# Two engines with priority for the first down projection's evictions, a three-operand token norm and urgent splits of v

## The chip, the cores and the metric

The kernel runs on one core of a Trainium2 chip. The core has a matrix engine (TensorE, "PE" in the profile, its weight loads "PEld"), a vector engine (VectorE, "DVE"), an activation engine (ScalarE, "ACT"), a general engine (GpSimd, "POOL") and a queue engine that only starts DMAs here (SyncE, "SP"). They share an on-chip memory with 128 partitions, and a smaller accumulation memory (PSUM) into which TensorE writes, in eight banks of 128 x 512 float32. The metric is the device time of one execution in microseconds. Before the change it is 1038.46 us, the median of three runs from 1038.11 to 1038.9.

## The reference

Eight batches of eight heads, 576 tokens, head width 64, go through causal attention with a window of 128 tokens and a bias that falls linearly with distance. The heads side by side make 4608 rows of 512 numbers, and these go through a bilinear feed-forward layer:

```python
scores = np.matmul(q, k.transpose(0, 1, 3, 2)) / np.sqrt(D)
rel = pos[:, None] - pos[None, :]
scores = np.where((rel >= 0) & (rel < 128), scores - slopes * np.abs(rel), -1e9)
attn = np.exp(scores - scores.max(-1)); attn = attn / (attn.sum(-1) + 1e-9)
x = (attn @ v).transpose(0, 2, 1, 3).reshape(4608, 512)
out = ((x @ w_a) * (x @ w_b)) @ w_out        # w_a, w_b: 512 x 1536, w_out: 1536 x 512
```

All inputs and the output are float32. The kernel keeps float32 accuracy by writing an operand as the sum of two float16 numbers, a high and a low half, and by adding three products of halves.

## The kernel before, in words

Work goes batch by batch. Tokens lie along the free axis as two halves of 288 (HT), and the 512 model columns as four blocks of 128 partitions (NPAIR and NE are both 4: four pairs of heads, four blocks of output rows). The 1536 hidden columns are twelve blocks (NF). While TensorE does the feed-forward layer of batch b, the attention of batch b+1 is woven into it.

**The first batch** has a path of its own. `first_attention` computes batch 0's attention while the weights arrive, and the generators `up_weights` and `down_weights` put the weights into form in between: operations on int32 and float32 columns (L100 to L161) that end with the halves in `wup` and `wdn`. At the end of `first_attention`, a pair's part of x is multiplied by its normalisation (L600), squared (`square_x`, L404 to L411), and the four pairs' squares go to `hidden_scale` (L488 to L505): two matmuls with ones per operand (L496, one for 512 tokens and one for 64) sum the squares over partitions into the PSUM tiles `n_ps`; maxima of these give `st.g`, the power of two that scales the hidden values. In `square_x` POOL adds the squares of pairs 1 and 2 onto those of pair 0 (L409), and those of pair 3 stay a second operand.

Then `first_batch` weaves `first_up` (twelve blocks, four groups of twelve matmuls each, L805, evicted by ACT at L758 and by DVE at L760, where DVE needs `st.g`) and `first_down` with the attention of batch 1 and with the rest of the weights. `first_down` goes over the two halves of tokens (t = 0, 1): four PSUM banks `dn_ps` collect 36 matmuls each (L787), in turns, so that all four are finished at almost the same time. Then each is scaled by `oi` and written to a `row` tile by ACT (L791) and sent to memory by a DMA that ACT issues (L792). `row` has two buffers. The five banks that `bank()` hands out in turns hold the next `dn_ps` tiles, and after t = 1 the `up_ps` tiles of batch 1.

**Order of work.** Until the end of `first_batch` only SP's order is written out by hand; the other engines' is set by a scheduler, which takes what is ready by a modelled time and by priority (`tc.high_priority(offset=PRIO)` moves work ahead, PRIO is 2000). From batch 1 on TensorE's order is the program's too. An engine executes its queue strictly in order: an instruction that waits holds up everything behind it, DMA issues included.

**Other names.** `split_v` (L279) makes `vhl`, the two halves of v for a pair of heads: ACT the high half (L282) and DVE the low one (L283); the matmuls L482 multiply it with the transposed probabilities `pT` into `x_ps`. `sc_ps` are scores (L361), `t` and `mn` their reduction by DVE (L369) and exponential by ACT (L370), `phl` the normalised halves (L382, L383), `qkh`, `qkl` the halves of q and k (L308, L325), `vsq` the squares of the next batch's v (L265). PSUM pools: `ps_at`, three banks, holds `sc_ps`, `n_ps`, the weight norms `wn_ps` and small sums; `ps_ef` (three) and `ps_ch` (two) the rest. `rc` tiles (three buffers) hold hidden values.

Of the kernel before, what the change touches and what calls it, by code (L numbers as in the profile page):

```python
# [13 lines left out]
BF16 = mybir.dt.bfloat16  # L14
# [3 lines left out]
AF = mybir.ActivationFunctionType  # L18
ALU = mybir.AluOpType
# [27 lines left out]
def attention_then_bilinear_ffn(ctx: ExitStack, tc: tile.TileContext, qT, kT, vP, w_a, w_b, w_out, rel, slopes2, outT):  # L47
# [231 lines left out]
    def split_v(st, p):  # L279

        vhl = work.tile([P, 2, VCOLS], F16, tag="vhl", name="vhl", bufs=2)
        act.activation(vhl[:, 0, :], st.v[:, p, :], AF.Copy, scale=st.sv)  # L282
        vec.scalar_tensor_tensor(out=vhl[:, 1, :], in0=st.v[:, p, :], scalar=st.sv, in1=vhl[:, 0, :], op0=ALU.mult, op1=ALU.subtract)  # L283
        return vhl

    def load_plain_qk(b, p):
# [110 lines left out]
            act.activation(x[:, c:c + w], ps[:, 0:w], AF.Copy, scale=scale)  # L397
        square_x(p, st, x)

    def square_x(p, st, x, add=True):  # L400

        if p == 0:
            act.activation(st.xq, x, AF.Square, scale=1.02)
            st.squares = [st.xq]  # L404
        else:
            sq = work.tile([P, S], BF16, tag="sq", name="sq")
            act.activation(sq, x, AF.Square, scale=1.02)  # L407
            if add:
                pool.tensor_tensor(out=st.xq, in0=st.xq, in1=sq, op=ALU.add)  # L409
            else:  # L410
                st.squares.append(sq)  # L411

    B12 = 7

# [90 lines left out]
    def first_attention(weights, rate):  # L505
# [74 lines left out]
        def pv(p, pt):  # L580
# [18 lines left out]
            for n, (c, w) in enumerate(halves_of_x):  # L599
                vec.scalar_tensor_tensor(out=x[:, c:c + w], in0=xp[n][:, 0:w], scalar=st.sv, in1=r[:, c:c + w], op0=ALU.mult, op1=ALU.mult)  # L600
            yield
            square_x(p, st, x, p < NPAIR - 1)
            yield

        bias(0)
# [142 lines left out]
    def new_hidden():  # L748
        return work.tile([P, 2, HT], F32, tag="rc", name="rc", bufs=3)
# [29 lines left out]
    def first_down(b, oi, h):  # L779

        started["down"] = b
        for t in range(2):
            pss = [bank("dn_ps") for _ in range(NE)]
            for f in range(NF):
                for e in range(NE):
                    for n, (wi, hi) in enumerate(((0, 0), (0, 1), (1, 0))):
                        pe.matmul(pss[e][:, 0:HT], wdn[:, f, wi, e * P:(e + 1) * P], h[:, f, t, hi, :], start=(f == 0 and n == 0), stop=(f == NF - 1 and n == 2))  # L787
                yield
            for e in range(NE):
                o = row()  # L790
                act.activation(o, pss[e][:, 0:HT], AF.Copy, scale=oi)  # L791
                act.dma_start(outT[e * P:(e + 1) * P, b * S + t * HT:b * S + (t + 1) * HT], o)  # L792

    def row():
        return work.tile([P, HT], F32, tag="row", name="row", bufs=2)
# [234 lines left out]
```

## Time and profile before

| what | value |
| --- | --- |
| three runs | 1038.11, 1038.46, 1038.9 us |
| the profiled execution | 1035.06 us, of which its span is 1033.3 us |
| mean granted TensorE clock | 0.98 |
| PE busy | 980.7 us, 95% of the span |
| DVE busy | 677.4 us, 66% |
| ACT busy | 647.5 us, 63% |
| POOL busy | 315.6 us, 31% |

Times inside the program are microseconds from the span's start. A row of the timeline gives the start, the busy time, the engine, the line and operation, what is written from what, and how many instructions the row holds; square brackets at its end give the idle time of that engine before the row and what ended it. A row of a table by stretches gives the start and end of the stretch, its length, each engine's busy time (with its count of instructions), the granted TensorE clock as a share of full speed, and the DMA engines' share and rate. By stage, `first_attention` ends at about 66 us, `first_up` runs to about 172 us (the last eviction of `up_ps` at L758 begins at 171.6 us), the evictions of `first_down` begin at 193.1 and at 221.4 us, and from 235 us on batches 1 to 7 run.

### The profile page before, as it was taken

The page shows a single profiled execution, that of the slowest core. Times are in us where ns is not written, and L with a number is a line of the kernel's source. Part 1 is how long each engine was busy: PE and PEld are TensorE (multiplying, and loading weights), DVE is VectorE, ACT ScalarE, POOL GpSimd, SP SyncE. Part 2 cuts the span into 40 slices and gives each one's busy share as a digit, 9 for nine tenths or more (in the row PEclk, how much of TensorE's full clock was granted, in tenths as well). Part 3 has the DMA queues.
Part 4 walks back from the last instruction along what each step waited for, and adds up shares of the span by engine and source line. Part 5 has one row for each costly group of instructions (what it writes and reads, how often), then busy time and mean ns, then how long its engine had stood idle before and what let it go on. Part 6 is the DMA issues. An engine that isn't in the chain of part 4 may idle for free.

```text
span 1033.3 us, 23882 instructions
## 1 busy us (share of the span) xinstructions
PE 980.7 (95%) x9325; PEld 754.8 (73%) x9325; DVE 677.4 (66%) x1880; ACT 647.5 (63%) x1672; POOL 315.6 (31%) x348
## 2 busy tenths in 40 slices
PE   8789979889999899889999999999999999999998
PEld 6556657667777677667777777777777778787776
DVE  5889988355778656985767667765776576534430
ACT  7977778556667756667666676667666765423321
POOL 3544562000368205880222212321223012221100
PEclk8899989999999999999999999999999999999999
DMA  8335733462543532435434743453624732200001
GB/s 344 125 111 195 251 86 73 100 155 58 123 88 86 145 74 56 87 80 153 88 65 86 184 90 65 88 116 115 124 52 99 173 65 42 48 31 11 1 13 35
DMA packets 148433, 102.83 MB, mean 100 GB/s; under 512 B 120032, under 2 KB 128352, under 8 KB 147296
## 3 DMA queue, kind: packets, MB, share of 16 engines
q1 hardware_dynamic: 138816, 91.77, 35.8%
q10 hardware_dynamic: 9504, 9.54, 2.9%
q8 instruction: 73, 1.20, 0.5%
q14 instruction: 40, 0.33, 0.1%
HBM read 48.33 MB, written 9.44 MB: 56 GB/s over the span
## 4 chain that ended last, share of the span: by engine, by line
PE 58%; DVE 15%; DMA 12%; ACT 7%; issue 3%; POOL 3%; SPq 2%; ACTq 0%; DVEq 0%; POOLq 0%
PE ch L805 16%; PE p L805 13%; PE dn_ps L901 11%; PE up_ps L805 10%; PE x_ps L482 4%; DMA pT<-phl 3%; DVE phl L383 3%; PE sc_ps L365 2%; DVE t L369 2%; ACT phl L382 1%; DMA v<-in_vP 1%; DMA qk<-in_kT 1%; DMA qst<-qkl 1%; DMA qst<-qkh 1%; DMA qkl<-qkl 1%
## 5 line engine op out<-in xcount | busy, mean ns | idle before, releaser
L805 PEld LDWEIGHTS <-wup 128*128 128x128 f16 x4212 | 407.7, 98 | 126.9 <-issue 18.6
L901 PE MATMUL dn_ps<-h,wdn 128*128 128x288 f16 x2016 | 256.8, 287 | 2.5 <-DVE h L799 2.5
L805 PE MATMUL ch<-xs,wup 128*128 128x288 f16 x1584 | 230.0, 287 | 6.7 <-DVE rc L865 4.3
L901 PEld LDWEIGHTS <-wdn 128*128 128x128 f16 x2016 | 193.9, 98 | 56.6 <-issue 3.7
L805 PE MATMUL up_ps<-xs,wup 128*128 128x288 f16 x1440 | 188.1, 289 | 6.0 <-ACT row L791 3.7
L805 PE MATMUL p<-xs,wup 128*128 128x288 f16 x1188 | 178.7, 287 | 0.0
L860 POOL TENSOR_TENSOR rc<-rc,row 128x288 f32<-128x288 f32 x66 | 64.5, 978 | 254.0 <-DVE row L858 235.6
L370 ACT ACTIVATE t<-t,mn 128x192 f32<-128x192 f32 (+2 forms) x252 | 107.4, 428 | 38.6 <-DVE mn L369 36.9
L383 DVE SCALAR_TENSOR_TENSOR phl<-t,rin,phl 128x192 f16<-128x192 f32 (+2 forms) x252 | 103.9, 447 | 34.5 <-ACT phl L382 34.5
L798 ACT CAST h<-rc 128x576 f16<-128x576 f32 x96 | 64.3, 669 | 64.0 <-DVE rc L865 33.1
L382 ACT ACTIVATE phl<-t,rin 128x192 f16<-128x192 f32 (+2 forms) x252 | 88.6, 426 | 19.4 <-DMA pT<-phl 11.4
L799 DVE TENSOR_TENSOR h<-rc,h 128x576 f16<-128x576 f32 x90 | 72.2, 802 | 26.4 <-ACT h L798 25.9
L369 DVE CUSTOM_DVE_ANT_0 t<-sc_ps,bias,neg 128x192 f32<-128x192 f32 (+2 forms) x216 | 74.3, 389 | 13.4 <-PE sc_ps L365 9.6
L842 ACT ACTIVATE row<-ch,g 128x288 f32<-128x288 f32 x66 | 32.9, 498 | 66.0 <-PE ch L805 66.0
L417 DVE TENSOR_TENSOR xs<-v,xs 128x576 f16<-128x576 f32 x51 | 52.5, 1044 | 28.4 <-ACT xs L416 27.9
L135 POOL TENSOR_TENSOR wup<-wup,wdn 128x512 int32<-128x512 int32 x36 | 56.9, 1602 | 33.7 <-issue 5.6
L906 ACT ACTIVATE row<-dn_ps,oi 128x288 f32<-128x288 f32 x56 | 27.7, 495 | 60.4 <-PE dn_ps L901 60.4
L837 DVE TENSOR_TENSOR rc<-p,rc 128x288 f32<-128x288 f32 x66 | 30.0, 454 | 45.5 <-PE p L805 41.5
L409 POOL TENSOR_TENSOR xq<-xq,sq 128x576 bf16<-128x576 bf16 x23 | 34.1, 1481 | 83.7 <-ACT sq L407 83.3
L482 PE MATMUL x_ps<-pT,vhl 128*64 128x128 f16 (+3 forms) x1176 | 47.8, 233 | 5.4 <-DVE vhl L283 2.6
L482 PEld LDWEIGHTS <-vhl 128*64 128x64 f16 (+1 forms) x1176 | 44.1, 112 | 11.2 <-issue 3.9
L365 PEld LDWEIGHTS <-qst 128*64 128x64 f16 x864 | 30.8, 110 | 27.8 <-issue 24.6
(139 smaller groups left out, 1301.1 us busy)
## 6 DMA issues: line engine op xcount, KB each, us to landing
v<-in_vP SPq DMA_DIRECT2D x8, 1280.0 KB, 6.6
out<-row ACTq DMA_DIRECT2D x64, 144.0 KB, 1.8
qk<-in_qT SPq DMA_DIRECT2D x28, 288.0 KB, 3.9
qk<-in_kT SPq DMA_DIRECT2D x28, 288.0 KB, 4.4
wdn<-in_w_a SPq DMA_DIRECT2D x12, 512.0 KB, 4.0
wdn<-in_w_b SPq DMA_DIRECT2D x12, 512.0 KB, 4.9
wdn<-in_w_out SPq DMA_DIRECT2D x12, 512.0 KB, 4.8
qst<-qkh SPq DMA_DIRECT2D x24, 144.0 KB, 2.4
```

Of the source, the lines that this page charges most:

```text
L135: pool.tensor_tensor(out=t[:, m, :], in0=t[:, m, :], in1=low[:, m, :], op=ALU.add)
L369: vec.tensor_tensor_reduce(out=t[:, c:c + w], in0=ps[:, c:c + w], in1=o.bias[:, WIN - w:WIN], scale=-0.125 if o.b == 1 else o.neg, scalar= ...
L370: act.activation(t[:, c:c + w], t[:, c:c + w], AF.Exp, bias=o.mn[:, n:n + 1], scale=-1.0, accum_out=o.sm[:, n:n + 1])
L382: act.activation(phl[:, 0, pc:pc + w], e, AF.Copy, scale=s)
L383: vec.scalar_tensor_tensor(out=phl[:, 1, pc:pc + w], in0=e, scalar=s, in1=phl[:, 0, pc:pc + w], op0=ALU.mult, op1=ALU.subtract)
L417: vec.tensor_tensor(out=xs[:, n, 1, :, :], in0=src, in1=xs[:, n, 0, :, :], op=ALU.subtract)
L482: pe.matmul(xp[oc // 512][64 * h:64 * h + 64, o0:o0 + w], vt[0:rows, c:c + 64], probs(pt, rows, blocks, h), start=(n == 0 and first), stop ...
L798: act.copy(h[:, f, :, 0, :], hid)
L799: eng.tensor_tensor(out=h[:, f, :, 1, :], in0=hid, in1=h[:, f, :, 0, :], op=ALU.subtract)
L805: pe.matmul(ps[:, 0:HT], wup[:, a[0], a[1], wi, k, :], xs[:, b, xi, k, :], start=(first and n == 0), stop=(last and n == len(ks) - 1), ski ...
L860: pool.tensor_tensor(out=x0, in0=x0, in1=mid, op=ALU.mult)
L901: pe.matmul(ps[:, 0:HT], wdn[:, f, wi, e * P:(e + 1) * P], h[:, f, t, hi, :], start=(m == 0 and n == 0), stop=(m == NF - 1 and n == 2))
```

## The change

Three functions are edited.

- `split_v`: as long as batch 1's x is unfinished (`states` has no entry 1), both operations are recorded with priority. That holds for batch 1's four pairs.
- `square_x`: `first_attention` keeps the squares of pair 2 in a tile of their own in the pool `first`, and no longer adds them on POOL; those of pair 3 stay in `work` as before. `hidden_scale` then has three operands for batch 0, and so two more matmuls.
- `first_down`: evictions have priority; blocks 0 and 2 are evicted by ACT, blocks 1 and 3 by DVE; blocks 0 and 1 go to `row`, blocks 2 and 3 into the halves of one `rc` tile. The four DMAs stay in ACT's queue.

```diff
 def split_v(st, p):
     vhl = work.tile([P, 2, VCOLS], F16, tag="vhl", name="vhl", bufs=2)
-    act.activation(vhl[:, 0, :], st.v[:, p, :], AF.Copy, scale=st.sv)
-    vec.scalar_tensor_tensor(out=vhl[:, 1, :], in0=st.v[:, p, :], scalar=st.sv, in1=vhl[:, 0, :], op0=ALU.mult, op1=ALU.subtract)
+    with tc.high_priority(offset=PRIO) if not states.get(1) else ExitStack():
+      act.activation(vhl[:, 0, :], st.v[:, p, :], AF.Copy, scale=st.sv)
+      vec.scalar_tensor_tensor(out=vhl[:, 1, :], in0=st.v[:, p, :], scalar=st.sv, in1=vhl[:, 0, :], op0=ALU.mult, op1=ALU.subtract)
...
-def square_x(p, st, x, add=True):
+def square_x(p, st, x, keep=None):
     if p == 0:
         act.activation(st.xq, x, AF.Square, scale=1.02)
         st.squares = [st.xq]
+    elif keep:
+        sq = keep.tile([P, S], BF16, tag="sq", name="sq")
+        act.activation(sq, x, AF.Square, scale=1.02)
+        st.squares.append(sq)
     else:
         sq = work.tile([P, S], BF16, tag="sq", name="sq")
         act.activation(sq, x, AF.Square, scale=1.02)
-        if add:
-            pool.tensor_tensor(out=st.xq, in0=st.xq, in1=sq, op=ALU.add)
-        else:
-            st.squares.append(sq)
+        pool.tensor_tensor(out=st.xq, in0=st.xq, in1=sq, op=ALU.add)
...   (first_attention)
-            square_x(p, st, x, p < NPAIR - 1)
+            square_x(p, st, x, first if p == 2 else work if p == 3 else None)
...   (first_down)
+            more = new_hidden()
             for e in range(NE):
-                o = row()
-                act.activation(o, pss[e][:, 0:HT], AF.Copy, scale=oi)
+                o = row() if e < 2 else more[:, e - 2, :]
+                with tc.high_priority(offset=PRIO):
+                    if e % 2:
+                        vec.tensor_scalar(out=o, in0=pss[e][:, 0:HT], scalar1=oi, scalar2=None, op0=ALU.mult)
+                    else:
+                        act.activation(o, pss[e][:, 0:HT], AF.Copy, scale=oi)
                 act.dma_start(outT[e * P:(e + 1) * P, b * S + t * HT:b * S + (t + 1) * HT], o)
```

In the changed program lines are shifted: by 1 from L282 on (L283 becomes L284, L369 and L370 become L370 and L371), and in and after `first_down` by 3 to 9 (L787 becomes L790, L791 becomes L798 on DVE and L800 on ACT, L792 becomes L801, L805 becomes L814). The scheduler's order differs on TensorE, ACT, DVE and POOL from the last part of `first_attention` to the start of batch 1; SP's order is the same, and from batch 1's up projection on TensorE's is too. Three places:

ACT at the end of `first_down`'s second half (t = 1), before. The tiles `dn_ps_2470` to `2473` are blocks 0 to 3.

```order
L791 ACTIVATE row_2812<-dn_ps_2470,oi_2123 128x288
L370 ACTIVATE t_2758,sm_2647<-t_2758,mn_2646 128x128
L791 ACTIVATE row_2815<-dn_ps_2471,oi_2123 128x288
L370 ACTIVATE t_2758,sm_2647<-t_2758,mn_2646 128x192
L792 DMA out_0<-row_2812 128x288
L792 DMA out_0<-row_2815 128x288
L370 ACTIVATE t_2799,sm_2647<-t_2799,mn_2646 128x192 x2
L816 COPY rc_2827<-up_ps_2828 128x288
L265 ACTIVATE vsq_2985,vs_2984<-v_2783 128x640
...
L791 ACTIVATE row_2818<-dn_ps_2472,oi_2123 128x288
L325 ACTIVATE qkh_2778<-qk_2649,own_2862 128x1152
L265 ACTIVATE vsq_2987,vs_2984<-v_2783 128x640
L791 ACTIVATE row_2821<-dn_ps_2473,oi_2123 128x288
```

And now:

```order
L800 ACTIVATE row_2813<-dn_ps_2470,oi_2124 128x288
L371 ACTIVATE t_2758,sm_2647<-t_2758,mn_2646 128x128
L371 ACTIVATE t_2758,sm_2647<-t_2758,mn_2646 128x192
L800 ACTIVATE rc_2812<-dn_ps_2472,oi_2124 128x288
L801 DMA out_0<-row_2813 128x288
L801 DMA out_0<-row_2816 128x288
L801 DMA out_0<-rc_2812 128x288
L371 ACTIVATE t_2799,sm_2647<-t_2799,mn_2646 128x192 x2
L801 DMA out_0<-rc_2812 128x288
L825 COPY rc_2826<-up_ps_2827 128x288
L265 ACTIVATE vsq_2984,vs_2983<-v_2783 128x640
```

Blocks 1 and 3 have left ACT, and block 2's eviction stands ahead of the squares of v (`vsq`), behind which it stood.

DVE ahead of the low halves of v for batch 1's first two pairs, before:

```order
L131 TENSOR_SCALAR wup_120<-wdn_121 128x2x512
L760 SCALAR_TENSOR_TENSOR rc_1649<-rc_1649,g_782,up_ps_1679 128x288
L133 SCALAR_TENSOR_TENSOR wup_120<-wdn_121,wup_120 128x2x512
L283 SCALAR_TENSOR_TENSOR vhl_1674<-v_823,sv_1615,vhl_1674 128x640
L283 SCALAR_TENSOR_TENSOR vhl_1870<-v_823,sv_1615,vhl_1870 128x640
```

And now:

```order
L131 TENSOR_SCALAR wup_120<-wdn_121 128x2x512
L284 SCALAR_TENSOR_TENSOR vhl_1675<-v_824,sv_1616,vhl_1675 128x640
L284 SCALAR_TENSOR_TENSOR vhl_1871<-v_824,sv_1616,vhl_1871 128x640
L763 SCALAR_TENSOR_TENSOR rc_1650<-rc_1650,g_783,up_ps_1680 128x288
L133 SCALAR_TENSOR_TENSOR wup_120<-wdn_121,wup_120 128x2x512
```

One up eviction and one operation of a weight block (L133) have moved behind the two splits; all else that stands ahead of them is the same set of instructions as before.

TensorE where the squares of pair 2 enter the norm, before (the sums `n_ps_770` and `n_ps_774` begin here, with pairs 0 to 2 already added):

```order
L482 MATMUL x_ps_750<-pT_161,v_145 64x64 x4
L496 LDWEIGHTS ones16_73
L496 MATMUL n_ps_770<-xq_147,ones16_73 128x512
L496 LDWEIGHTS ones16_73
L496 MATMUL n_ps_774<-xq_147,ones16_73 128x64
L361 MATMUL sc_ps_835<-qkl_820,qkh_819 64x64 x2
L361 MATMUL sc_ps_835<-qkl_820,qkh_819 64x128 x2
```

And now (the sums began with `xq` some fifty rows earlier, ahead of `sc_ps_836`, which is the old `sc_ps_835`):

```order
L362 MATMUL sc_ps_896<-qkl_821,qkh_820 64x192 x4
L594 MATMUL rin_ps_725<-ident_131,rin0_722 64x64 x16
...
L499 MATMUL n_ps_769<-sq_716,ones16_73 128x512
L499 LDWEIGHTS ones16_73
L499 MATMUL n_ps_774<-sq_716,ones16_73 128x64
L156 LDWEIGHTS ones16_73
L156 MATMUL wn_ps_926<-wdn_121,ones16_73 128x256
```

Scores of batch 1 (`sc_ps_836`, `sc_ps_896`) and a weight norm (`wn_ps_926`) now stand ahead of the last `x_ps` matmuls of batch 0, with the two sums `n_ps` open among them in two of the pool's three banks.

## The prediction

> **What bounds the kernel now.** I read the table by stretches first, cut where the program's stages end.
>
> ```profile
> core 0: us, PE busy (x) PEld busy (x) DVE busy (x) ACT busy (x) POOL busy (x), PEclk, DMA share, GB/s
> 53.00:82.00 29.00, 24.31 (x235) 17.40 (x234) 22.14 (x55) 21.17 (x52) 11.30 (x13) 0.94 0.38 146
> 82.00:139.00 57.00, 52.16 (x435) 38.55 (x432) 55.98 (x103) 44.30 (x93) 33.91 (x29) 1.00 0.56 189
> 139.00:148.00 9.00, 4.17 (x49) 3.07 (x50) 8.30 (x12) 5.82 (x14) 9.00 (x5) 0.65 0.00 0
> 193.00:235.00 42.00, 34.91 (x310) 25.40 (x309) 19.19 (x76) 23.86 (x70) 1.77 (x2) 0.92 0.61 145
> 235.00:1033.30 798.30, 777.29 (x7444) 606.41 (x7439) 501.64 (x1426) 474.19 (x1240) 224.73 (x250) 1.00 0.36 82
> ```
>
> From 235 us TensorE is busy 777.29 of 798.30 us at full clock, in an order that the change leaves alone: that part can only shift as a whole. Everything is decided before 235 us, in three places: 193 to 235, where TensorE is idle for 42.00 - 34.91 = 7.1 us and its clock falls to 0.92 while DVE and ACT are busy below 24 us; 139 to 148, idle for 4.8 us at 0.65; and 82 to 139, where DVE is busy 55.98 of 57.00 us, so that DVE's queue sets the pace there.
>
> Second, TensorE's timeline through `first_down`, to see what ends each gap:
>
> ```profile
> 160.01 1.65 PE L482 MATMUL x_ps<-pT,vhl 128*64 128x128 f16 x42
> 193.66 2.75 PE L787 MATMUL dn_ps<-h,wdn 128*128 128x288 f16 x21 [0.20 <-ACT row L791]
> 199.99 2.32 PE L787 MATMUL dn_ps<-h,wdn 128*128 128x288 f16 x9 [3.21 <-ACT row L791]
> 202.40 2.10 PE L482 MATMUL x_ps<-pT,vhl 128*64 128x128 f16 x42
> 204.43 3.11 PE L787 MATMUL dn_ps<-h,wdn 128*128 128x288 f16 x24
> 221.96 3.10 PE L805 MATMUL up_ps<-xs,wup 128*128 128x288 f16 x24 [0.73 <-ACT row L791]
> 230.03 4.77 PE L805 MATMUL up_ps<-xs,wup 128*128 128x288 f16 x24 [2.94 <-ACT row L791]
> 235.18 10.46 PE L805 MATMUL up_ps<-xs,wup 128*128 128x288 f16 x84
> ```
>
> Each large gap ends with an ACT eviction (L791). After each the matmuls are slow: nine took 2.32 us, where 24 undisturbed ones take 3.11.
>
> Third, ACT's timeline, for why the evictions are late:
>
> ```profile
> 193.13 0.86 ACT L791 ACTIVATE row<-dn_ps,oi 128x288 f32<-128x288 f32 x2
> 193.64 1.78 ACTq L792 DMA_DIRECT2D out<-row  x2
> 199.44 0.50 ACT L791 ACTIVATE row<-dn_ps,oi 128x288 f32<-128x288 f32 x1 [3.43 <-DMA out<-row]
> 201.14 0.50 ACT L791 ACTIVATE row<-dn_ps,oi 128x288 f32<-128x288 f32 x1 [0.77 <-DMA out<-row]
> 221.43 0.48 ACT L791 ACTIVATE row<-dn_ps,oi 128x288 f32<-128x288 f32 x1
> 227.20 0.74 ACT L265 ACTIVATE vsq<-v 128x640 bf16<-128x640 f32 x1 [2.84 <-DMA v<-in_vP]
> 229.50 0.48 ACT L791 ACTIVATE row<-dn_ps,oi 128x288 f32<-128x288 f32 x1
> 237.56 1.16 ACT L308 ACTIVATE qkl<-qk 128x1152 bf16<-128x1152 f32 x1 [1.85 <-DMA qk<-in_kT]
> 239.16 0.38 ACT L816 COPY rc<-up_ps 128x288 f32<-128x288 f32 x1
> ```
>
> At t = 0 the third eviction waits 3.43 us for a buffer, until an output DMA has landed; at t = 1 it stands behind a square of v that waits 2.84 us for the load of v.
>
> **Term 1, evictions at t = 0.** The gaps are 0.20 + 3.21 = 3.41 us. Slow matmuls behind the second: nine at the undisturbed rate take 9/24 x 3.11 = 1.17 us, so 2.32 costs 1.15; the 42 of `x_ps` at 202.40 took 2.10 against 1.65 at 160.01, another 0.45. Together 5.0 us. With four buffers no eviction waits for a landing. ACT is left with two evictions of 0.50 us, a DMA issue between them (the pair at 193.64 took 1.78, so 0.9 each), and DVE with two. For those no row exists; the nearest is a DVE read of a 128x288 PSUM tile:
>
> ```profile
> L760 DVE SCALAR_TENSOR_TENSOR rc<-rc,g,up_ps x24: 433/502/517, 74.3 to 173.7; 128x288 f32<-128x288 f32 x24
> ```
>
> That has one more tensor operand, and bounds the new one between 0.43 and 0.52; I take 0.50, as on ACT. DVE's queue has 42.00 - 19.19 = 22.8 us free in the stretch. The DMAs wait on ACT for DVE's half: behind them stand two exponentials (L371) and the q/k split. The wait is one DVE eviction, 0.5 us, plus whatever runs on DVE at that moment; no TensorE instruction needs those exponentials within it. All 5.0 us go if the third block is free 1.7 us after TensorE starts into the second half (its 21 matmuls took 2.75 us, and the banks come in turns of 3). Eviction, issue, eviction on ACT is 0.50 + 0.9 + 0.50 = 1.9 from the end, so up to 0.2 us may stay. Bounds 3.4 (gaps alone) to 5.0; I take 5.0, since the full rate is the rule away from gaps.
>
> **Term 2, evictions at t = 1.** The gap of 2.94 and the slow 24 behind it (4.77 - 3.10 = 1.67) make 4.61 us. The 0.73 us stays: the first eviction's place behind ACT's work is unchanged. Block 2 now stands ahead of `vsq`, blocks 1 and 3 are on DVE. The load of v is as late as before, so the wait for v remains on ACT, and what is late next is the next copy of an up group. With five banks each group needs the eviction of the fifth before it. The 84 matmuls at 235.18 are seven groups of 1.49 us; counted from the first up group, they are groups 7 to 13, and group 12 starts at 235.18 + 5 x 1.49 = 242.65. It needs the copy (L816) of group 7, ended at 239.16 + 0.38 = 239.54 and held there by a load of q and k. TensorE 4.61 us earlier would be there at 238.04: 1.5 us given back. The load is issued once the q/k split has freed its buffer, and that split stands behind one L791 fewer, 0.5 us earlier, which leaves 1.0. Gain 3.6; bounds 4.61 - 1.5 = 3.1 and 4.6.
>
> **Term 3, urgent splits of v.** The waits on TensorE, and what stands around them on DVE and POOL:
>
> ```profile
> 141.19 0.28 PE L482 MATMUL x_ps<-pT,vhl 128*64 128x128 f16 x4 [2.24 <-ACT vhl L282]
> 145.10 2.75 PE L482 MATMUL x_ps<-pT,vhl 128*64 128x128 f16 x38 [2.64 <-DVE vhl L283]
> 143.15 3.73 DVE L283 SCALAR_TENSOR_TENSOR vhl<-v,sv,vhl 128x640 f16<-128x640 f32 x2
> L133 DVE SCALAR_TENSOR_TENSOR wup<-wdn,wup 128x1024 int32<-128x1024 int32 x10 | 14.5, 1447 | 0.0
> ```
>
> The splits start at 143.15 because DVE's queue is full to there. The order now puts one L133 (1.447) and one L760 (0.502) behind them and leaves the rest ahead: 1.95 us earlier. Those two are not lost, but nobody waits for them in that time: TensorE has matmuls of `x_ps` to do. The upper bound is both waits and the slow clock: 2.24 + 2.64 + (2.75 - 38/42 x 1.65) = 6.1 us; the lower is nothing, if DVE only swaps which work is late. I take 1.9, the price of what was moved.
>
> **Term 4, the norm.**
>
> ```profile
> 59.31 1.26 PE L591 MATMUL rin_ps<-ident,rin 64*64 64x64 f32 x36 [1.70 <-DVE v L600]
> 62.38 2.12 PE L482 MATMUL x_ps<-pT,v 128*64 128x128 f32 x28 [0.96 <-ACT rin L595]
> 66.52 0.53 PE L496 MATMUL n_ps<-xq,ones 128*128 128x512 bf16 x2 [2.03 <-POOL xq L409]
> 61.41 3.37 POOL L135 TENSOR_TENSOR wup<-wup,wdn 128x512 int32<-128x512 int32 x2 [0.18 <-ACT wdn L141]
> 64.74 1.73 POOL L409 TENSOR_TENSOR xq<-xq,sq 128x576 bf16<-128x576 bf16 x1
> 61.20 4.13 DVE L150 SCALAR_TENSOR_TENSOR wup<-wup,sup 128x512 f16<-128x512 f32 x3
> 68.57 0.23 DVE L369 CUSTOM_DVE_ANT_0 t<-sc_ps,bias 128x64 f32<-128x64 f32 x1 [2.38 <-PE sc_ps L361]
> 72.09 0.36 DVE L369 CUSTOM_DVE_ANT_0 t<-sc_ps,bias 128x192 f32<-128x192 f32 x1 [1.46 <-PE sc_ps L361]
> 78.29 0.52 DVE L760 SCALAR_TENSOR_TENSOR rc<-rc,g,up_ps 128x288 f32<-128x288 f32 x1 [1.60 <-PE up_ps L805]
> 80.48 0.36 DVE L369 CUSTOM_DVE_ANT_0 t<-sc_ps,bias 128x192 f32<-128x192 f32 x1 [1.01 <-PE sc_ps L361]
> ```
>
> The add on POOL waits behind two L135, TensorE waits 2.03 us for it, the scores queued behind it come late, and DVE idles 2.38 us for them. The add goes; its price is two more matmuls with ones, 0.53 us for such a pair. Since DVE sets the pace from 82 us, what counts is DVE's idle time here: 2.38 + 1.46 + 1.60 + 1.01 = 6.45 us, the upper bound. Against it: the two sums now hold two of three banks, so batch 1's scores and a weight norm go through the third in turn. If one hand-over stands behind the three L150, it costs up to 4.13 us, the lower bound. I take 2.0: the first idle time, 2.38, less the pair, rounded up from 1.85 because some of the later ones shrink.
>
> **Sum.** 5.0 + 3.6 + 1.9 + 2.0 = 12.5 us. The profiled execution took 1035.06, which makes 1022.6 for its like. The median of the runs is 3.40 above it, and the changed kernel is timed by such runs: 1038.46 - 12.5 = 1026.0 us.
>
> On the clock, the Trainium skill ("TensorE: Matmul & The Clock Gate", "What's actually happening") says that TensorE falls to half rate only after a whole idle window of about 3.4 us, counted freely. By that rule neither gap of `first_down`, 3.21 and 2.94, must throttle; the rows of slow matmuls right behind both, and the granted 0.92, disagree with it as a threshold. By the rule the 3.3 us of slow matmuls in terms 1 and 2 need not belong to the gaps.
>
> **Rivals.**
>
> A. DVE's pace stays: what terms 3 and 4 move earlier only waits elsewhere, as 55.98 busy of 57.00 us suggests, since the work itself is not less. Against: DVE idles before 82. Terms 1 and 2 alone: 1038.46 - 8.6 = 1029.9.
>
> B. All the idle goes: upper bounds everywhere, 5.0 + 4.6 + 6.1 + 6.4 = 22.1, so 1016.4. For: the three waits feed one another. Against: DVE's full queue.
>
> C. The slow matmuls come whether the gaps are there or not (a clock that follows TensorE's average load, not the gap ahead). Then 1.15 + 0.45 + 1.67 = 3.3 us are not won: 1029.3. Against: from 235 us on, with hardly a gap, the clock is 1.00.
>
> D. Slower: one bank for batch 1's scores. With `n_ps` in the other two until the last square is summed, each of three tiles waits until DVE has read the one before, and if each read stands behind a group of L150 (4.13), that is 12.4 us late, and two L150 and four L369 that now precede the norm's maxima add 2 x 1.38 + 4 x 0.36 = 4.2. It decides once the lateness exceeds the other terms' 10.5 us: all of it gives 1038.46 + 16.6 - 10.5 = 1044.6. Against: DVE reads of scores have stood between such groups so far, and one hand-over is likelier than three.
>
> E. No change: the evictions were the last wait only by a little, and loads of v, q and k, as late as before, take their place on ACT: within a microsecond of 1038.5.
>
> **Chances.** Forecast 0.46, A 0.18, B 0.12, C 0.10, E 0.08, D 0.06. Some 0.2%, about 2 us, is what a measurement of this kernel can tell from no change. Forecast, A, B and C are faster by more: 0.86; E is the same, 0.08; D slower, 0.06. The likeliest's own range is 1021 to 1030, with the sum at 17 and at 8.5 us. The range of 8 in 10 is 1018 to 1035: what is left out is E, D and about half of B, 0.20.
>
> **What would show it.** Term 1: no wait of TensorE above 0.5 us between 185 and 205 on an eviction, and no ACT eviction that waits for an output DMA. Term 2: no 2.94 us gap behind the first up groups of batch 1, but one of about 1 us some eight groups later, ended by a copy (L825) behind the load of q and k. Clock 1.00 in both, or C is right. Term 3: DVE's two splits 1.9 us earlier relative to the up matmuls ahead of them, the waits at `x_ps` 4.9 us in sum before and about 3 after. Term 4: scores before 66 us, DVE idle 66 to 82 less by 2; a TensorE wait on `t` (L370) above 3 us ahead of `wn_ps` would be D. The time from the first up group of batch 1 to the end must stay what it was but for term 2's gaps; if that changes, the ground of the sum is wrong.

## The result and the profile after

The changed kernel takes 1030.83 us, the median of six runs from 1027.8 to 1032.97; the kernel before, run beside it and earlier, 1037.91 (1035.77 to 1038.9). The ratio is 0.9931, with a 95% interval from 0.9911 to 0.9952: 7.2 us faster, 5.0 to 9.2. The forecast was 1026.0, 12.5 below before, with a range of 1018 to 1035. The profiled execution took 1027.8 us, with a span of 1026.0, against 1035.06 and 1033.3.

The table by stretches of the changed kernel (same columns and cuts as before):

```profile
53.00:82.00 29.00, 24.72 (x244) 18.28 (x243) 24.68 (x66) 21.55 (x55) 10.44 (x16) 0.94 0.23 84
82.00:139.00 57.00, 49.10 (x412) 36.77 (x410) 53.78 (x93) 42.73 (x91) 26.43 (x22) 1.00 0.63 217
139.00:148.00 9.00, 7.51 (x90) 5.47 (x89) 9.00 (x12) 5.43 (x13) 8.99 (x5) 1.00 0.20 39
193.00:235.00 42.00, 39.65 (x378) 30.31 (x376) 23.36 (x82) 25.80 (x75) 2.27 (x3) 1.00 0.52 132
```

Between 193 and 235 us TensorE is busy 39.65 us (34.91 before) at full clock. Between 82 and 139 it is busy less than before, 49.10 against 52.16. Its timeline at the places of the four terms:

```profile
65.85 0.61 PE L156 MATMUL wn_ps<-wdn,ones 128*128 128x256 bf16 x4 [3.14 <-DVE mn L370]
66.39 3.74 PE L485 MATMUL x_ps<-pT,v 128*64 128x128 f32 x28
126.34 1.63 PE L814 MATMUL up_ps<-xs,wup 128*128 128x288 f16 x12 [2.33 <-DVE rc L763]
132.77 1.63 PE L814 MATMUL up_ps<-xs,wup 128*128 128x288 f16 x12 [2.31 <-DVE rc L763]
143.60 1.56 PE L485 MATMUL x_ps<-pT,vhl 128*64 128x128 f16 x38 [1.49 <-DVE vhl L284]
195.67 1.63 PE L485 MATMUL x_ps<-pT,vhl 128*64 128x128 f16 x42
197.23 3.11 PE L790 MATMUL dn_ps<-h,wdn 128*128 128x288 f16 x24
214.49 3.10 PE L814 MATMUL up_ps<-xs,wup 128*128 128x288 f16 x24 [0.45 <-ACT row L800]
232.52 3.10 PE L814 MATMUL up_ps<-xs,wup 128*128 128x288 f16 x24 [1.75 <-ACT rc L825]
```

The gap of 3.21 us in the middle of the down projection is gone, and so is the one of 2.94 us in the up groups; a new one of 1.75 us stands where term 2 said, behind a copy. New too are waits of 3.14, 2.33 and 2.31 us in the first batch.

To say where time went, I use four instructions that every kernel here has, the small matmuls `qtot` (L319, L320 after) at the start and the end of the stretch with `first_down`, in batch 1, and at the same place of batch 2. Before:

```profile
170.63 0.17 PE L319 MATMUL qtot<-both,ones 128*128 128x2 bf16 x1
221.06 0.17 PE L319 MATMUL qtot<-both,ones 128*128 128x2 bf16 x1
255.74 0.18 PE L319 MATMUL qtot<-both,ones 128*128 128x2 bf16 x1
370.73 0.18 PE L319 MATMUL qtot<-both,ones 128*128 128x2 bf16 x1
```

After:

```profile
168.47 0.18 PE L320 MATMUL qtot<-both,ones 128*128 128x2 bf16 x1
213.87 0.17 PE L320 MATMUL qtot<-both,ones 128*128 128x2 bf16 x1
245.71 0.18 PE L320 MATMUL qtot<-both,ones 128*128 128x2 bf16 x1
363.24 0.18 PE L320 MATMUL qtot<-both,ones 128*128 128x2 bf16 x1
```

The stretches between them (call them A to E: up to the first, first to second, and so on, E to the end of the span) in all traces of this study, worked out in the same way, with the ratio of the runs:

| kernel | A | B: first_down | C | D | E | ratio (95%) |
| --- | --- | --- | --- | --- | --- | --- |
| before | 170.6 | 50.4 | 34.7 | 115.0 | 662.6 | 1 |
| before, again (c4) | 171.5 | 50.8 | 35.4 | 116.3 | 665.4 | (one run) |
| whole change | 168.5 | 45.4 | 31.8 | 117.5 | 662.8 | 0.9931 (0.9911 to 0.9952) |
| whole change, again (a1) | 170.1 | 45.4 | 32.5 | 117.7 | 664.3 | 0.9931 (0.9914 to 0.9948) |
| evictions alone (b1) | 170.5 | 51.7 | 33.9 | 118.1 | 663.9 | 1.0003 (0.9986 to 1.0020) |
| splits of v alone (b2) | 169.2 | 50.9 | 32.9 | 116.7 | 663.3 | 0.9995 (0.9980 to 1.0009) |
| norm alone (b3) | 170.3 | 45.8 | 34.5 | 118.0 | 663.8 | 0.9949 (0.9930 to 0.9967) |
| whole change without norm (c2) | 169.6 | 52.1 | 33.3 | 118.4 | 663.9 | 0.9994 (0.9974 to 1.0013) |
| one move on ACT (c1) | 168.7 | 45.3 | 33.5 | 114.7 | 662.7 | 0.9947 (0.9928 to 0.9967) |
| that move and evictions (c3) | 171.0 | 45.0 | 32.4 | 116.0 | 663.7 | 0.9933 (0.9909 to 0.9956) |
| whole change, sums open later (d1) | 168.5 | 51.8 | 31.5 | 117.7 | 666.9 | 1.0002 (0.9987 to 1.0016) |
| whole change, a copy first (d2) | 168.8 | 45.4 | 30.1 | 118.2 | 663.8 | 0.9907 (0.9885 to 0.9929) |
| whole change, layout first (d3) | 169.1 | 45.4 | 29.4 | 113.6 | 660.1 | 0.9806 (0.9781 to 0.9831) |
| two moves, nothing of the change (f1) | 172.2 | 45.2 | 32.8 | 112.5 | 658.3 | 0.9851 (0.9832 to 0.9871) |

Stretch A differs by up to 3.5 us between traces with the same order up to there (168.7 in c1, 172.2 in f1), so a difference in it says little. Each trace is one execution, and some were fast for their kernel: those of c1, b2, the whole change and before lie 5.9, 4.6, 3.0 and 2.9 us below the medians of their runs. So a difference of 2 or 3 us between two traces in C, D or E needs more than the table. B has two values, 45.0 to 45.8 and 50.4 to 52.1, and nothing in between.

### The profile page after: what moved, and what is told of

The parts are those of the page before. It is cut to its first block, busy times and chain, and to the rows that moved or that the text cites. A ratio compares the mean times of both kernels' runs of the same rounds, so it can differ in the third digit from the quotient of the medians.

```text
span 1026.0 us, 23881 instructions
## 1 busy us (share of the span) xinstructions
PE 976.3 (95%) x9327; PEld 752.4 (73%) x9327; DVE 682.9 (67%) x1884; ACT 644.7 (63%) x1668; POOL 310.0 (30%) x347
## 4 chain that ended last, share of the span: by engine, by line
PE 55%; DVE 10%; DMA 9%; ACT 6%; POOL 4%; issue 3%; SPq 1%; ACTq 0%; DVEq 0%; POOLq 0%
PE ch L814 16%; PE p L814 12%; PE dn_ps L910 12%; PE up_ps L814 8%; DMA pT<-phl 4%; PE x_ps L485 3%; DVE phl L384 3%; PE sc_ps L366 2%; ACT phl L383 1%; PE dn_ps L790 1%; DMA qst<-qkh 1%; DMA qkl<-qkl 1%; DMA qk<-in_kT 1%; DVE t L370 1%; DMA qst<-qkl 1%
## 5 line engine op out<-in xcount | busy, mean ns | idle before, releaser
L814 PEld LDWEIGHTS <-wup 128*128 128x128 f16 x4212 | 406.5, 98 | 128.3 <-issue 21.4
L814 PE MATMUL ch<-xs,wup 128*128 128x288 f16 x1584 | 228.9, 286 | 7.8 <-DVE rc L874 5.3
L814 PE MATMUL up_ps<-xs,wup 128*128 128x288 f16 x1440 | 185.9, 288 | 7.9 <-DVE rc L763 4.6
L814 PE MATMUL p<-xs,wup 128*128 128x288 f16 x1188 | 178.0, 286 | 0.0
L371 ACT ACTIVATE t<-t,mn 128x192 f32<-128x192 f32 (+2 forms) x252 | 107.4, 427 | 34.2 <-DVE mn L370 33.1
L384 DVE SCALAR_TENSOR_TENSOR phl<-t,rin,phl 128x192 f16<-128x192 f32 (+2 forms) x252 | 104.4, 450 | 31.5 <-ACT phl L383 31.3
L807 ACT CAST h<-rc 128x576 f16<-128x576 f32 x96 | 64.2, 669 | 61.3 <-DVE rc L874 32.8
L383 ACT ACTIVATE phl<-t,rin 128x192 f16<-128x192 f32 (+2 forms) x252 | 88.6, 425 | 16.6 <-DMA pT<-phl 8.6
L370 DVE CUSTOM_DVE_ANT_0 t<-sc_ps,bias,neg 128x192 f32<-128x192 f32 (+2 forms) x216 | 74.5, 390 | 13.8 <-PE sc_ps L366 13.7
L851 ACT ACTIVATE row<-ch,g 128x288 f32<-128x288 f32 x66 | 32.9, 498 | 65.9 <-PE ch L814 65.9
L135 POOL TENSOR_TENSOR wup<-wup,wdn 128x512 int32<-128x512 int32 x36 | 54.6, 1538 | 43.7 <-DVE wup L133 14.1
L414 POOL TENSOR_TENSOR xq<-xq,sq 128x576 bf16<-128x576 bf16 x22 | 31.6, 1438 | 76.5 <-ACT sq L413 76.2
L239 POOL TENSOR_TENSOR wa<-wup 128x512 f32<-128x512 f16 x24 | 31.1, 1298 | 62.9 <-DVE phl L384 62.1
L348 POOL TENSOR_SCALAR bias<-rel_sb,ninv,sl_sb 128x192 f32<-128x192 f32 x24 | 17.4, 724 | 108.4 <-DVE mn L370 108.4
```

The source lines that it names most:

```text
L135: pool.tensor_tensor(out=t[:, m, :], in0=t[:, m, :], in1=low[:, m, :], op=ALU.add)
L370: vec.tensor_tensor_reduce(out=t[:, c:c + w], in0=ps[:, c:c + w], in1=o.bias[:, WIN - w:WIN], scale=-0.125 if o.b == 1 else o.neg, scalar= ...
L371: act.activation(t[:, c:c + w], t[:, c:c + w], AF.Exp, bias=o.mn[:, n:n + 1], scale=-1.0, accum_out=o.sm[:, n:n + 1])
L383: act.activation(phl[:, 0, pc:pc + w], e, AF.Copy, scale=s)
L384: vec.scalar_tensor_tensor(out=phl[:, 1, pc:pc + w], in0=e, scalar=s, in1=phl[:, 0, pc:pc + w], op0=ALU.mult, op1=ALU.subtract)
L807: act.copy(h[:, f, :, 0, :], hid)
```

## The experiments

### One part at a time

The first four runs: the whole change again, and each of its parts alone, as the hunks of the diff.

> The changed kernel, nothing edited, for a second trace. In the first trace the second half of the down projection is over 7.19 us earlier than before, batch 1's up projection 10.03 us, and 10.33 us at 326 us; then a wait of 3.63 us for the laid-out q and k (2.67 before) and slow matmuls behind it take 2.84 us back. Theory A, an accident of that execution (the landing of one DMA): this trace has a wait near 2.7 us there, no slow matmuls, a span near 1023. Theory B, a work that does not move with the rest (a transfer): the wait is again above 3.3 us with slow matmuls behind it, span near 1026. Time 1028 to 1033 in both.

It was between the two theories. The wait for the laid-out q and k was 2.81 us, near the 2.7 of A, but a second of 1.32 us followed, and the matmuls behind were slow; the span was 1030.0. The ratio, 0.9931, is the same.

> Only the evictions of the first down projection (two engines, priority, four buffers) on top of the kernel before; norm and splits of v as before. Theory: terms 1 and 2 carry the whole gain. Up projection of batch 1 earlier by 5.0 to 5.8 at its start and by 8 to 9 us at its twelfth group, with a gap of 1 to 1.8 us behind the load of q and k; time 6 to 9 us below before, the 6 if the wait ahead of batch 2's scores takes 2.8 back. Rival: the evictions need the other parts, gain below 4.

Nothing was gained: 1.0003 (0.9986 to 1.0020), 1039.36 against 1039.37 us. Stretch B became longer, 51.7 against 50.4 us. TensorE's one large wait in it, of the evictions-alone kernel:

```profile
201.28 2.90 PE L482 MATMUL x_ps<-pT,vhl 128*64 128x128 f16 x42 [3.55 <-DMA pT<-phl]
```

The wait for an eviction is gone, and TensorE waits 3.55 us for the transposed probabilities `pT` instead, with slow matmuls behind (2.90 us for 42, where 1.65 is the undisturbed time). On ACT three of the four DMA issues are slow:

```profile
193.43 0.35 ACTq L798 DMA_DIRECT2D out<-row  x1
193.91 1.25 ACTq L798 DMA_DIRECT2D out<-row  x1
195.25 1.13 ACTq L798 DMA_DIRECT2D out<-rc  x1
196.48 1.38 ACTq L798 DMA_DIRECT2D out<-rc  x1
```

> Only the priority of the splits of v, on top of the kernel before. Theory, term 3: the low halves start 1.9 us earlier (two operations of DVE less ahead of them), and all behind them up to the down projection moves by 1.5 to 1.9; time 1.5 to 2 us below before if nothing takes it back. Rival: DVE's queue only swaps what is late, the up evictions behind the splits hold TensorE instead: 0 at the down projection, no difference in time.

No difference: 0.9995 (0.9980 to 1.0009). The waits at `x_ps` were 2.24 and 2.92 us, as before (2.24 and 2.64). The two instructions that stand behind the splits in the changed kernel are still ahead of them here: their move belongs to the norm's part, not to the priority.

> Only the third operand of the token norm, on top of the kernel before. In the changed kernel's trace a weight norm waits 3.14 us for DVE's read of the scores (one bank left for them) and the first up eviction is only 0.16 us earlier than before. Theory: the hand-over eats the whole of term 4 by itself, so here too: the wait of about 3 us ahead of the weight norm, slow matmuls of x behind it, first up eviction within 0.5 us of before, time within 1 us of before. Rival: the norm alone gains 2 us as forecast, and it is the other parts' order that takes it away.

Here both were wrong. The wait of 3.14 us for DVE's read is there, so the hand-over is real, but the norm alone gains 5.3 us: 0.9949 (0.9930 to 0.9967), 1034.04 us. And it gains them in stretch B, 45.8 against 50.4 us, 120 us behind the norm, with the evictions as before. So the missing addition is not what pays.

### What the norm's part moves

The norm's part changes the work ahead of 170 us, and the scheduler's order behind it comes out differently. On ACT in stretch B, the squares of q and k of batch 2's second pair (L308, L309 after) stand ahead of the normalisation `phl` (L382, L383) in the kernel before, in b1, b2, c2 and d1, and behind it in the whole change and in b3. Before, ACT:

```profile
187.19 1.16 ACT L308 ACTIVATE qkl<-qk 128x1152 bf16<-128x1152 f32 x1 [4.36 <-DMA qk<-in_kT]
189.78 1.49 ACT L382 ACTIVATE phl<-t,rin 128x192 f16<-128x192 f32 x4 [0.45 <-DVE rin L379]
```

and SP, which sends the transposes when `phl` is done:

```profile
191.78 4.91 SPq L388 DMA_TRANSPOSE pT<-phl  x1
```

After, ACT:

```profile
182.56 1.49 ACT L383 ACTIVATE phl<-t,rin 128x192 f16<-128x192 f32 x4 [0.45 <-DVE rin L380]
187.40 1.16 ACT L309 ACTIVATE qkl<-qk 128x1152 bf16<-128x1152 f32 x1 [3.35 <-PE sc_ps L366]
```

and SP:

```profile
184.56 5.28 SPq L389 DMA_TRANSPOSE pT<-phl  x1
```

Before, ACT waits 4.36 us for a load with ready work behind it, and the transposes go out at 191.78 us, just ahead of the four output transfers of t = 0 that begin at 193.64. After, they go out at 184.56, and the squares wait behind them (for the same load, which lands at 187.30 us there, though their row names TensorE).

To test that alone, one instruction was moved, with nothing of the change: the squares of that one pair are put behind the last instruction of the normalisation. On ACT this one instruction changes its place, on DVE the one that reads its result; all else is in the order of before.

```diff
-            act.activation(phl[:, 0, pc:pc + w], e, AF.Copy, scale=s)
+            last_phl[0] = act.activation(phl[:, 0, pc:pc + w], e, AF.Copy, scale=s)
...
-            with behind():
+            with tc.issue_after(last_phl[0].ins) if i == 4 else behind():
                 nxt = squares(i + 1)
```

> The kernel before with one instruction moved on ACT (and its follower on DVE): the squares of q and k of batch 2's second pair, which wait for a load until 187 us, stand behind the normalisation of the probabilities instead of ahead of it; nothing else differs. The runs of single parts showed that the norm alone gains 5 us and that its order has just this move, so that the transposed probabilities are sent at 186 instead of 192 us. Theory: this move is the gain. TensorE's idle time of 3 us in the middle of the first down projection goes, also with ACT alone evicting into two buffers, the stage from 170 to 221 us is 4.6 us shorter, the time 4 to 5 us below before. Rival: the gain of the norm part is the missing addition and the earlier scores: no more than 1 us here.

0.9947 (0.9928 to 0.9967), 1032.60 against 1038.45 us, and B is 45.3 us. One moved instruction gives what the norm's part gives, without any of it. That rests on the runs and on B; D and E of this trace, an execution of 1026.66 us, are those of a fast one. ACT of this kernel, where evictions go one after the other into two buffers as before:

```profile
189.18 0.89 ACT L793 ACTIVATE row<-dn_ps,oi 128x288 f32<-128x288 f32 x2 [0.24 <-PE dn_ps L789]
192.39 0.50 ACT L793 ACTIVATE row<-dn_ps,oi 128x288 f32<-128x288 f32 x1 [0.64 <-DMA out<-row]
193.22 0.49 ACT L793 ACTIVATE row<-dn_ps,oi 128x288 f32<-128x288 f32 x1
```

The third eviction waits 0.64 us for its buffer, not 3.43, since the output transfers land sooner. The first fence gives their time from issue to landing at t = 0 before: first the two transfers that ACT issues at 193.64 and 194.08 us, then the two that it issues from 201.22 us on, when the transposes have landed (201.21).

```profile
DMA to landing us min/median/max: 5.7/6.3/7.0
DMA to landing us min/median/max: 1.7/1.8/1.8
```

The second gives all four of the kernel with one move, then all four of the evictions alone.

```profile
DMA to landing us min/median/max: 1.8/2.4/2.6
DMA to landing us min/median/max: 5.1/5.9/6.9
```

So the wait for a buffer goes with the transposes: outputs issued 1.9 to 4.9 us after SP starts on them land after 5.1 to 7.0 us, those issued 5.1 us after or later land after 1.7 to 2.6. That these share the DMA engines is the plain reading; what exactly they share, the traces don't show. Transposes are not the only thing that makes outputs late: at t = 1 they land about when the outputs are issued, v's load is in flight instead, and the first two outputs take 5.1 to 6.3 us in all three kernels.

> The same move with the new evictions on top; norm and splits of v as before. Theory: evictions count only once the transposes are early, and then mostly at the start of batch 1's up projection: 6 to 7.5 us below before, as the whole change. Rival: evictions are worth nothing at any place: the same as with the move alone.

0.9933 (0.9909 to 0.9956), as the whole change, 1031.03 us. B is 45.0 us, no shorter than without the new evictions; C is 32.4 against 33.5. The interval does not tell it from the move alone.

> The changed kernel with the two-operand norm of before: new evictions and urgent splits only. The order on ACT there has the squares ahead of the normalisation again. Theory: nothing is gained, within 2 us of before, with TensorE waiting some 3.5 us for transposed probabilities at about 200 us. Rival: evictions and splits are worth 2 us or more together.

0.9994 (0.9974 to 1.0013), with a wait of 3.84 us for `pT`: evictions and splits without the norm's order are worth nothing.

> The kernel before, nothing edited, for a second trace. In its first trace batch 2's first scores waited 2.67 us with no slow matmuls behind, while all five other traces lost 1.7 to 3.1 us more there. If that first trace was the exception, the stretch from 256 to 371 us is 1.5 to 3 us longer here; if the loss belongs to arriving earlier, it is as long as in the first trace (115.0 us from one sum of squares to the other).

One run of 1041.09 us, with a span of 1039.3. The stretch D is 116.3 us against 115.0, its wait 2.63 us and a second of 0.73, and slow matmuls behind. So the first trace of before was a good one, by 1.3 us in D and 2.8 in E, and part of the 2.5 us that the changed kernel seemed to lose in D is that. The other 1.2 us lie within what D varies by (114.7 to 118.4), and a good part of it depends on the clock: the last section shows how.

### Three edits of the changed kernel

The sums of the norm opened later, to take the 3.14 us away:

```diff
-            st.squares.append(sq)
+            st.squares.insert(0 if p == 2 else 2, sq)
```

> The changed kernel with another order of the three operands of the norm: the sums begin with pair 2's squares, so that the two PSUM tiles of the sums open some 9 us later and batch 1's first scores have all three banks. In the changed kernel a weight norm waited 3.14 us there for DVE's read of the scores, with slow matmuls of x behind it (3.74 us for 28, 2.12 before). Theory: this hand-over is what ate term 4; without it the wait of 3.14 us is below 1 us, the first up eviction comes 1 to 3 us earlier, and DVE's idle time from 53 to 82 us falls; of that 0 to 2 us reach the end, since DVE sets the pace after 82 us. Rival: the wait only moves, same time as the changed kernel (ratio to before 0.993). The order of the scheduler changes with it, and if the normalisation falls behind the squares of q and k again, 5 us are lost.

1.0002 (0.9987 to 1.0016). The wait of 3.14 us is gone, and the first up eviction on DVE starts at 72.08 us instead of 78.13, but stretch A is 168.5 us, against 168.5 and 170.1 with the wait: as far as single traces of A can tell, term 4 is worth nothing at its end even without the hand-over. And the last sentence of the expectation came true: in this order the squares stand ahead of the normalisation again, TensorE waits 3.94 us for `pT`, B is 51.8, and the whole gain is lost.

The copy of batch 1's seventh up group ahead of the squares that wait for a load at 230 us (one instruction moved on ACT, by recording these squares later and behind the copy):

```diff
+                if i == 6:
+                    with tc.issue_after(copied[0].ins):
+                        nxt = squares(i + 1)
```

> The changed kernel with one instruction moved on ACT: the squares of q and k that wait for a load at 230 us stand behind the copy of batch 1's seventh up group instead of ahead of it. Theory: the wait of 1.75 us (2.21 in the second trace) for that copy, the give-back of term 2, goes, and the start of batch 1's next stage is 1.5 to 2 us earlier; in time 0 to 2 us below the changed kernel, ratio to before 0.991 to 0.993. Rival: the squares become late for the next q and k and take it back.

0.9907 (0.9885 to 0.9929), 1028.31 us. The wait of 1.75 us is gone and C is 30.1 us, 1.8 to 2.5 shorter than in the two traces of the whole change. That is the give-back of term 2, shown in the trace by taking it away; in the time, the interval overlaps that of the whole change.

SP's order in the step of each batch's second pair, from batch 2 on, where the third pair is laid out by four copies inside the chip: the first two (`laid` is the second) now go ahead of the next two loads, and the other two follow between these.

```diff
-            load(i + 2)
+            with tc.issue_after(nxt.laid.ins) if p == 1 and nxt and nxt.b > 1 else ExitStack():
+                load(i + 2)
```

> The changed kernel with an order on SP: where a batch's scores of the second pair are laid out, the two copies inside the chip are issued ahead of the next loads of q and k, which shared the DMA engines with them. In all traces TensorE waits there at batch 2 (1.7 to 3.6 us plus up to 1.3) and, by less, in later batches, and slow matmuls follow in most. Theory: the copies land 1 to 2 us sooner, the stretch from 246 to 363 us shrinks from 117.5 to about 115, and the whole by 2 to 4 us: ratio to before 0.989 to 0.991. Rival: the copies are slow by themselves: no change, 0.993.

0.9806 (0.9781 to 0.9831), 1018.43 against 1038.29 us, faster than either theory allowed. In batch 2's up projection, where the scores of batch 3's third pair are woven in (the expectations call them batch 2's), the whole change has

```profile
344.70 0.22 PE L366 MATMUL sc_ps<-qkh,qst 128*64 128x64 f16 x2 [3.63 <-DMA qkh<-qkh]
346.11 7.71 PE L814 MATMUL up_ps<-xs,wup 128*128 128x288 f16 x48
```

and this kernel

```profile
341.52 0.22 PE L366 MATMUL sc_ps<-qkl,qst 128*64 128x64 f16 x2 [1.07 <-DVE phl L384]
342.06 6.04 PE L815 MATMUL up_ps<-xs,wup 128*128 128x288 f16 x48
```

The wait for the copies is gone, the matmuls behind run at full rate (6.04 us for 48, 7.71 in the whole change), D is 113.6 and E 660.1 us. In C it is 2.4 us shorter too, since the scheduler, with SP's order changed, put the same squares as in d2 behind a copy. The spans account for 8.4 us of the difference to the first trace of the whole change and for 12.4 to the second (1030.0 less 1017.6); the medians differ by 12.4.

The last run puts the two orders on the kernel before, with nothing of the change.

> The kernel before with nothing of the change: only the move of the one instruction on ACT (squares of q and k behind the normalisation, 0.9947 by itself) and the order on SP (layout copies ahead of the next loads, in the second pair of each batch). Theory: the two orders are independent and add up: 0.9947 - (0.9931 - 0.9806) = 0.982, some 19 us below before, and the new evictions, the splits and the norm are worth no more than 2 us beside them. Rival: the order on SP pays only with the new evictions, whose output transfers leave earlier: 0.988 or above.

0.9851 (0.9832 to 0.9871), 1022.47 us, between the two; the sum of the two orders, 0.982, lies just below the interval. So the whole change with SP's order (d3) is 0.9851 - 0.9806, some 4.5 us, faster than the two orders alone, more than the 2 us that I expected. The traces show where most of it may lie: in C, 29.4 us against 32.8. In both kernels the scheduler has put the squares of C behind copies, but here TensorE still waits for ACT's evictions of t = 1, and in d3 it has no such wait:

```profile
225.39 1.63 PE L808 MATMUL up_ps<-xs,wup 128*128 128x288 f16 x12 [2.67 <-ACT row L794]
227.65 1.63 PE L808 MATMUL up_ps<-xs,wup 128*128 128x288 f16 x12 [0.62 <-ACT row L794]
```

That is what term 2 was to remove. The split of the 4.5 us rests on one trace each, and the two ratios on different chips.

## Why the prediction was right, and where it was not

The sign held, and the time lies in the range; but the sum was 12.5 us and 7.2 came, and of its four terms one held by its own steps. That the time fell into the range is largely luck: the norm's part alone gains 5.3 us (b3), by a move that is in no term, and the evictions and splits without it gain nothing (c2). With it they add 1.9 us by the ratios of b3 and the whole change, whose intervals overlap.

**The reading of the bounds** was right on where: stretch B gave 5.0 us and C 2.1 to 2.8, and D and E shifted with them, within 3 us. It failed in the sentence "Each large gap ends with an ACT eviction": true of the rows, but a row names what came last, and in the run where no eviction was waited for, the transposed probabilities were there only at 201.28 us, 1.3 us after the eviction's gap had ended before (199.99).

**Term 1 (5.0 us).** B became 5.0 us shorter, by another cause. "With four buffers no eviction waits for a landing" and "All 5.0 us go" were wrong as a step: with the evictions alone nothing of it went, since the transposes were late next (3.55 us). The signs that the prediction named for this term, no wait for an eviction and no eviction that waits for an output, are there in that run too, without any gain. I had looked for what is behind the eviction on ACT and on DVE, and not for what TensorE needs next from SP's queue. The row that would have told it is SP's 191.78, with 4.91 us of issue and TensorE's `x_ps` at 202.40, right behind the gap. The 5 us came from the move of the squares of q and k, which the orders of the two programs show and the prediction did not price.

**Term 2 (3.6 us).** Right in its mechanism and place: a gap behind the copy of group 7, held by the load of q and k. The give-back was 1.75 and 2.21 us instead of 1.0: the half microsecond from the split's earlier place did not come. The gain in C was 2.8 and 2.1 us, and the part of it that the evictions make is less sure: 0.8 and 1.1 us in C by b1 against before and c3 against c1, and up to 3.4 by d3 against f1, where the give-back is gone too. The slow matmuls in its price (1.67 us) are not there in every execution of the kernel before: b2, which has the same gap, 2.89 us at 228.15, ran at full rate behind it.

**Term 3 (1.9 us)** was nothing. By itself the priority leaves the waits at `x_ps` as they were. In the two traces of the whole change the splits start at 141.65 and 143.26 us on DVE, before at 143.15 and 143.50: no earlier beyond what A varies by. The waits there fall from 4.88 to 1.49 us, and 2.33 and 2.31 us appear ahead of them, where the up evictions on DVE are late. The norm alone, without the priority, has the same three waits (2.35, 2.31 and 1.48 us), so this too is its order. That is rival A: DVE's work is not less, and TensorE waits elsewhere.

**Term 4 (2.0 us)** was nothing either. The hand-over of rival D happened once (3.14 us for DVE's read, with slow matmuls behind it, 3.74 us for 28 against 2.12), and its absence in d1 gave nothing back that stretch A shows. Nor did the up evictions start earlier: the first on DVE begins at 78.13 us, 74.30 before (the 0.16 us in the expectation of b3 compares it with a later one, at 78.29). "What counts is DVE's idle time here" was wrong: DVE was busy 2.5 us more from 53 to 82 us (24.68 against 22.14), and 2.2 less from 82 to 139 (53.78 against 55.98).

**Rivals.** A, the evictions alone at 1029.9, is near the measured 1030.83, and for the right reason as far as terms 3 and 4 go; but its own ground, terms 1 and 2 from the evictions, fell with b1. B's and D's times are outside what was measured, and E's ground, that a transfer takes the evictions' place, is what b1 shows, only with the transposes and not the loads that I named. C did not come: with the gaps gone, the granted clock from 193 to 235 us is 1.00 and the slow matmuls are gone with them; behind other gaps, in D, they are there.

## What to carry to other kernels

A wait that a profile names is the one that came last; before it is priced, list what the waiting engine needs next, from the DMA queues too, and see how far behind that is. Where a scheduler sets the order, an edit is also a throw of the order elsewhere: test a part alone, and then the one moved instruction alone, before a gain is put down to what the edit is about. And an instruction that waits for a load, queued ahead of ready work whose result goes out by DMA, costs twice: by the wait, and by the transfers that then go out together.

## What the runs showed of the hardware that I had not expected

The issue of a DMA is not a fixed price on its engine: three of the four output transfers of the evictions-alone kernel at t = 0 took 1.13 to 1.38 us to issue, from 193.91 us on, and the first of them, just before, 0.35. SP was issuing the transposes until 196.39 us there, and the last of the three starts at 196.48. In the kernel with one move, SP was done with them at 189.40, and the outputs, issued from 189.71 on, took 0.34 to 0.40; they landed after 1.8 to 2.6 us, those of the evictions alone after 5.1 to 6.9. What makes an issue slow stays open.

The length of a gap does not by itself tell whether the matmuls behind it are slow. Of the evictions alone, behind a gap of 2.15 us:

```profile
241.22 4.75 PE L811 MATMUL up_ps<-xs,wup 128*128 128x288 f16 x24 [2.15 <-ACT rc L822]
```

and of the kernel with one move, behind 3.16 us:

```profile
222.72 1.63 PE L807 MATMUL up_ps<-xs,wup 128*128 128x288 f16 x12 [3.16 <-ACT row L793]
```

The first are slow (24 take 3.10 us at full rate), the second at full rate. What tells them apart is where the gap lies in time. In the clock records of all traces, half clock comes in stretches of 3.41 us, or two or three times that, and within a trace their starts lie on one grid of 3.41 us; from trace to trace this grid lies elsewhere. The two gaps, cut at the grids of their traces:

```profile
237.81:241.22 3.41, 1.26 (x11) 0.88 (x9) 0.50 (x3) 2.41 (x7) 0.00 (x0) 1.00 0.46 107
241.22:244.63 3.41, 3.41 (x15) 2.17 (x15) 3.16 (x9) 2.64 (x7) 0.00 (x0) 0.50 0.15 34
```

```profile
218.09:221.50 3.41, 1.47 (x12) 1.04 (x11) 0.51 (x2) 1.61 (x6) 0.00 (x0) 1.00 0.41 156
221.50:224.92 3.42, 1.63 (x12) 1.17 (x12) 2.98 (x9) 3.42 (x9) 0.00 (x0) 1.00 0.13 45
224.92:228.33 3.41, 3.36 (x31) 2.47 (x31) 1.98 (x4) 3.41 (x11) 0.00 (x0) 1.00 0.60 168
```

The gap of 2.15 us lies whole in one window: TensorE is idle for 3.41 - 1.26 = 2.15 us of it, and the next window has half clock. The gap of 3.16 us is split: 1.94 us idle in one window, 1.79 in the next (a second short gap included), and the clock stays. From 60 us on, the 14 traces have 3881 such windows that are themselves at full clock. The next one was at half clock after all 56 in which TensorE was idle for 2.0 us or more, after 10 of the 32 with 1.75 to 2.0 us, and after none of the others. So a gap between 2 and 4 us may or may not cost a window at half clock, as it falls on the grid.

This is also what much of D's variation is. At the scores of batch 3's third pair, the first trace of before and the second (c4) wait nearly alike, 2.67 and 2.63 us:

```profile
349.98:353.39 3.41, 1.42 (x12) 0.89 (x10) 1.97 (x7) 3.41 (x11) 0.00 (x0) 1.00 0.57 178
353.39:356.81 3.42, 2.30 (x29) 1.78 (x30) 1.51 (x10) 2.34 (x9) 0.00 (x0) 1.00 0.35 93
```

```profile
352.70:356.11 3.41, 0.56 (x5) 0.17 (x3) 1.72 (x6) 3.41 (x9) 0.00 (x0) 1.00 0.56 141
356.11:359.53 3.42, 2.91 (x23) 1.90 (x24) 1.41 (x10) 1.78 (x8) 0.00 (x0) 0.50 0.11 37
```

TensorE idles 1.99 us of the window in the first and 2.85 in the second, and only behind the second is the clock half. D is 112.5 to 115.0 us in the four traces without half clock in it (before, c1, d3, f1), 116.0 to 118.0 in the seven with one such window, and 118.1 to 118.4 in the three with two (b1, c2, d2).

The three gaps above 3.5 us at that place (3.63, 3.56 and 3.79, of the whole change, d2 and b3) were all followed by slow matmuls: 48 in 7.71, 8.13 and 7.69 us, where 6.04 is the full rate. The Trainium skill ("TensorE: Matmul & The Clock Gate", "What's actually happening") has the clock fall after a whole idle window of about 3.4 us that runs freely. The length and the free running agree with the grid of 3.41 us; that the whole window must be idle does not, since 2.0 us of it were enough in every case here.
